# Loading and transposing the queries once, with the swapped half written by copies inside SBUF

## The chip, the cores and the metric

One core of one Trainium2 chip runs the whole program in a single launch. The metric is device time in microseconds (us) of that core. An engine is named as the profile does: PE is TensorE (PEld its weight loads), DVE is VectorE, ACT is ScalarE, POOL is GpSimd, SP is SyncE, which only issues DMAs here; SPq and ACTq are the queues of DMA issues of SP and ACT. HBM is the memory off the core, SBUF the memory on it, PSUM the memory that matmuls write to.

## The reference

Three layers in a row, all in float32, for 4 batches, 8 heads, 576 positions and a head width of 64 (model width 512):

```python
scores = scale * np.matmul(q, k.transpose(0, 1, 3, 2))
thresh = np.max(scores, axis=-1, keepdims=True) - tau
scores = np.where(scores >= thresh, scores, -1000000000.0)
...
attn = attn / (np.sum(attn, axis=-1, keepdims=True) + 1e-09)
return np.matmul(attn, v).astype(np.float32)
...
mixed = np.real(X).astype(np.float32)
u = x + mixed
...
ch = np.maximum(un @ w_ch1, 0.0) @ w_ch2
return (u + ch).astype(np.float32)
...
gate = 1.0 / (1.0 + np.exp(-gate_pre))
val = x @ w_val
return (gate * val @ w_out).astype(np.float32)
```

`X` is the Fourier transform of the attention's output over positions and model width, `un` is `u` normalised over the model width (512, with 2048 in the middle of the second layer), and `gate_pre` a causal convolution of 5 taps over positions.

The change touches only how the queries come to the first matmul.

## The kernel before, in words

**Stages.** The attention works on 16 pairs of heads (4 pairs to a batch). While it runs, TensorE's spare time is filled with other work of the attention and with the Fourier transform of the batches that are done, and the other engines convert the weights of the layer behind from 64-bit words to two float32r parts. When the attention's tiles end (about 380 us), the multilayer perceptron begins with its first block of columns, still mixed with the last batch's Fourier transform and the conversion of the rest of the weights; from about 505 us it and the gated output run matmul after matmul.

**Scores.** A pair has nine tiles of 128 query rows: four for each head and one that holds the last 64 rows of both. `emit_s` (L563) makes one tile's scores. The 576 keys of a head are held in two halves of 288: `kt[0:64, h]` holds keys 0 to 287 of head h (transposed, so that the 64 partitions are the head width), `kt[64:128, h]` keys 288 to 575. The matmul of a half contracts over the partitions that this half lies on, so the queries of the head must lie on partitions 0 to 63 and again on 64 to 127. Before the change both copies come from HBM: `qn` has an axis of 2 (`j`) that is loaded with the same rows twice, and a transpose of `[128 rows, 2 x 64]` gives both copies at once, in `qt[:, h]`.

**Loads.** `load_qk` (L179) issues nine DMAs per pair on SP, in this order: two for the keys (`kn`), one for the last 32 rows of each half of the keys (`tn`), two for the last 64 query rows (`tn` again, twice the same), four for the other 512 query rows (`qn`, two heads, each twice). For pair 0 the queries go through ACT's queue and are loaded once, and POOL copies them (L206). `nat_p` has one buffer, so the loads of a pair wait for the transposes of the pair before.

**Preparation.** `g_prep_qk` (L247) is a generator that makes a pair's `kt` and `qt`: four transposes of keys into one PSUM tile, copied out by DVE (L264); two transposes of 96 rows into a second, copied out by ACT (L271) and DVE (L272); then for each head four transposes of queries into a tile of its own, copied out by ACT with the scale (L279). At its `yield "sync"` it waits until its tiles are read, and issues the loads of the next pair.

**Order.** The attention is written step by step, two tiles a step, 72 steps and a few to drain. `ORDER` (L34) is the order of the pieces in a step: M0 and M1 are the row maxima (DVE, L585), E0 and E1 the exponentials (ACT, L592), K0 and K1 the masks (DVE, L602), S2 and S3 the scores of the next two tiles (PE, L573), N0 and N1 the division by the sum (POOL, L609), T0 and T1 the transposes of the probabilities (PE, L643), WD, WA, WP one operation of the weight conversion. F1 and F2 issue the ACT copies of the filler tiles that are ready, H1 to H3 the copies that follow on other engines. P1 and P2 call the filler (L678), which gives PE up to 1250 and 1350 ns of queued work, in this order of queues: `g_tail` (transposes of the probabilities' last columns, L623), the preparation of the next pair, the Fourier transform (L242), one mean, and the products with the values `g_pv` (L318). A filler tile needs room: its generator's `yield "room"` lets it go on only while at most one filler tile is open (`state["open"] <= 1`), so at most two tiles are started until copies have emptied them, however short they are. A pair's preparation is queued in the step in which the pair before begins, about four steps ahead of its first scores.

The lines that the prediction follows:

```python
def ready(g):
    ...
    if kind == "sync":
        return state["read"] >= put
    return state["open"] <= 1
...
queues = [(q_prep, q_tail, q_mean, q_pv, q_fft)[i] for i in QORD]
```

Where the whole `while` loop at L669 runs the preparation of pair 0, nothing else is on the engines.

Of the kernel before, what the change touches and what calls it, by code (L numbers as in the profile page):

```python
# [11 lines left out]
F32 = mybir.dt.float32  # L12
# [3 lines left out]
AF = mybir.ActivationFunctionType  # L16
# [5 lines left out]
B, H, S, D = 4, 8, 576, 64  # L22
# [4 lines left out]
MAIN, TAIL = 512, 64  # L27
HALF = S // 2
# [106 lines left out]
def attention_fft(tc, right, ps_f, a, u_d, dram, conv_w, hooks):  # L135
    nc = tc.nc
    PE, DVE, ACT, POOL, SP = nc.tensor, nc.vector, nc.scalar, nc.gpsimd, nc.sync
    left, right1 = ExitStack(), ExitStack()
    with ExitStack() as right2, ExitStack() as right2b, ExitStack() as right3, ExitStack() as right4, ExitStack() as scores, ExitStack() as turned:
        def pool(stack, name, bufs, side="right", **kw):  # L140
            return stack.enter_context(tc.tile_pool(name=name, bufs=bufs, side=side, **kw))
# [13 lines left out]
        nat_p = pool(left, "nat", 1, side="left")  # L155
# [3 lines left out]
        ident = id_p.tile([128, 128], F32, name="ident")  # L159
        tau = const.tile([128, 1], F32, name="tau_sb")  # L160
        atau = const.tile([128, 1], F32, name="atau")
        alpha = const.tile([128, 1], F32, name="alpha")
# [16 lines left out]
        def load_qk(p, second=SP):  # L179
            b, hs = p // NP, slice(2 * (p % NP), 2 * (p % NP) + 2)  # L180
            kn = nat_p.tile([128, 2, 2, 2, D], F32, tag="kn", name="kn")
            qn = nat_p.tile([128, 2, 4, 2, D], F32, tag="qn", name="qn")
            tn = nat_p.tile([96, 2, 2, D], F32, tag="tn", name="tn")
            k, q = a["k"][b, hs].rearrange("h (g p) d -> p h g d", g=2), a["q"][b, hs]
            for j in range(2):
                SP.dma_start(out=kn[:, j], in_=k[j * 128:j * 128 + 128])
            SP.dma_start(out=tn[0:32], in_=k[256:HALF])

            def queries(h, j):
                second.dma_start(out=qn[:, h, :, j], in_=q[h, 0:MAIN].rearrange("(t p) d -> p t d", p=128))  # L190

            def last_queries():
                for j in range(2):
                    second.dma_start(out=tn[32:96, :, j], in_=q[:, MAIN:S].rearrange("h p d -> p h d"))

            if second is SP:
                last_queries()
                for h in range(2):
                    for j in range(2):
                        queries(h, j)  # L200
            else:
                for h in range(2):
                    queries(h, 0)
                    if h == 0:
                        last_queries()
                    POOL.tensor_copy(qn[:, h, :, 1], qn[:, h, :, 0])  # L206
            nat[p] = tn, kn, qn

        def load_v(p):
# [22 lines left out]
        def fill_tile():  # L232
            state["open"] += 1
            return ps_f.tile([128, 512], F32, tag="f", name="f")

        def done(first, *then):

            evacs.append((first, then))
            state["put"] += 1
# [7 lines left out]
        def g_prep_qk(p):  # L247

            tn, kn, qn = nat.pop(p)
            kt = qk_p.tile([128, 2, HALF], F32, tag="kt", name="kt")  # L250
            qt = qk_p.tile([128, 2, S], F32, tag="qt", name="qt")

            yield "room"
            f = fill_tile()
            for h in range(2):
                for j in range(2):
                    o = (2 * h + j) * 128
                    PE.transpose(f[:, o:o + 128], kn[:, j, h].rearrange("p g d -> p (g d)"), ident)
                    yield 121.0
            fk = f.rearrange("p (h k) -> p h k", h=2)  # L260
            if KEYS_ACT:
                done(lambda: ACT.activation(kt[:, :, 0:256], fk, AF.Copy))
            else:
                done(lambda: None, lambda: DVE.tensor_copy(kt[:, :, 0:256], fk))  # L264
            yield "room"
            f = fill_tile()
            for h in range(2):
                PE.transpose(f[:, h * 96:h * 96 + 96], tn[:, h].rearrange("p g d -> p (g d)"), ident[0:96, 0:96])
                yield 121.0
            fv = f[:, 0:192].rearrange("p (h k) -> p h k", h=2)  # L270
            done(lambda fv=fv: ACT.activation(qt[:, :, MAIN:S], fv[:, :, 32:96], AF.Identity, scale=alpha[:, 0:1]),  # L271
                 lambda fv=fv: DVE.tensor_copy(kt[:, :, 256:HALF], fv[:, :, 0:32]))  # L272
            for h in range(2):
                yield "room"
                f = fill_tile()
                for t in range(4):
                    PE.transpose(f[:, t * 128:(t + 1) * 128], qn[:, h, t].rearrange("p g d -> p (g d)"), ident)
                    yield 121.0
                done(lambda f=f, h=h: ACT.activation(qt[:, h, 0:MAIN], f, AF.Identity, scale=alpha[:, 0:1]))  # L279
            yield "sync"  # L280
            if 0 < p < NPAIR - 1:
                load_qk(p + 1)
            kq[p] = (qt, kt)
# [273 lines left out]
        def force(ready):  # L557
            while not ready():
                flush()
                advance_side()  # L560
                fill(1.0)

        def emit_s(g):  # L563
            p, h, i = tiles[g]
            force(lambda: p in kq)
            qt, kt = kq[p]
            s = ps_s.tile([128, 2, 512], F32, tag="s", name="s")
            for hh in ((h,) if h < 2 else (0, 1)):
                q = slice(i * 128, i * 128 + 128) if h < 2 else slice(MAIN, S)
                o = slice(0, 128) if h < 2 else slice(hh * 64, hh * 64 + 64)  # L570
                for c in range(2):
                    w = slice(c * 64, c * 64 + 64)
                    PE.matmul(out=s[o, c, 0:HALF], lhsT=qt[w, hh, q], rhs=kt[w, hh, :], start=True, stop=True)  # L573
            sc[g] = s

        def p_view(g):
# [81 lines left out]
        LAG = 4  # L658
        SP.dma_start(out=ident, in_=a["ident"])
        load_qk(0, ACT)  # L660
        DVE.tensor_scalar(out=atau, in0=tau, scalar1=-1.0, scalar2=None, op0=ALU.mult)
        DVE.tensor_tensor(out=atau, in0=atau, in1=tau, op=ALU.max)
        for t in negs:
            for j in range(2):
                DVE.tensor_copy(t[:, j, 1:2], atau)
        DVE.tensor_scalar(out=alpha, in0=tau, scalar1=0.0, scalar2=float(D) ** -0.5,
                          op0=ALU.is_ge, op1=ALU.mult)
        q_prep.append(g_prep_qk(0))
        while q_prep:  # L669
            fill(1e9)  # L670
            flush()
        load_qk(1)
        emit_s(0)
        emit_s(1)

        spare = 0.0
# [6 lines left out]
        for u in range(NT // 2 + 3):  # L683
            t = 2 * u
            on = [x for x in (t, t + 1) if x < NT]
            state["tile"] = t
            for x in on:
                p, h, i = tiles[x]
                if h == 0 and i == 0 and p + 1 < NPAIR:
                    q_prep.append(g_prep_qk(p + 1))  # L690
                if h == 0 and i == 2:
                    if p == 0:
                        side.append(g_prep_v(0))
                    if p + 1 < NPAIR:
                        side.append(g_prep_v(p + 1))
# [30 lines left out]
            def S2():  # L726
                if t + 2 < NT: emit_s(t + 2)
# [816 lines left out]
```

## Time and profile before

| | us |
|---|---|
| median of 3 runs | 938.17 |
| lowest, highest | 937.34, 938.41 |
| span of the profiled execution, first to last instruction | 936.0 |

No time of its own is given for the profiled execution beyond its span, so durations are summed against 936.0, and the median is 938.17 - 936.0 = 2.2 us above it (other executions, timed around the whole launch).

| engine | busy us of 936.0 |
|---|---|
| PE | 884.3 (94%) |
| PEld | 708.0 (76%) |
| DVE | 553.5 (59%) |
| ACT | 451.2 (48%) |
| POOL | 368.0 (39%) |

How to read it: a matmul's duration in the profile is its latency, and matmuls overlap, so the cost of one in a row is the row's length divided by their count. A line of the timeline merges neighbouring instructions of one kind: start, length, engine, line of the kernel, operation, what it writes and reads, count, and in brackets the idle time of the engine before it and what ended it.

### The profile page before, as it was taken

What the parts mean: (1) busy time and instruction counts of PE and PEld (TensorE: products, weight loads), DVE (VectorE), ACT (ScalarE), POOL (GpSimd) and SP (SyncE); (2) the same over time, 40 slices, a digit from 0 to 9 for tenths busy, and PEclk for the clock granted to TensorE, in tenths of its full rate; (3) what the DMA queues carried; (4) which work ended last, traced back from release to release, by engine and by line L of the source; (5) the groups of instructions that cost most, each with busy time, mean ns of one, the idle gap of its engine ahead of it and who ended that gap; (6) DMA issues with size and microseconds to landing.
All of it is one profiled execution on the core that took longest, in us unless ns stands there. A gap on an engine that the chain in (4) does not pass through costs nothing. (4 is left out here: it accounts for less than half of the span.)

```text
span 936.0 us, 14888 instructions
## 1 busy us (share of the span) xinstructions
PE 884.3 (94%) x5232; PEld 708.0 (76%) x5232; DVE 553.5 (59%) x1240; ACT 451.2 (48%) x915; POOL 368.0 (39%) x451
## 2 busy tenths in 40 slices
PE   6988899999999999799988999999999999999998
PEld 4555576657665765488866999999999989998897
DVE  5888888888887767316577243442412275735750
ACT  3778777777777766526355123213211313224432
POOL 2465645584467545612553321312111011037421
PEclk9999999999999999999999999999999999999999
DMA  6775545556555732587259524212110050233111
GB/s 151 190 193 129 165 119 167 154 163 173 164 142 172 193 92 72 178 314 234 89 204 351 204 91 130 79 46 85 52 66 1 1 178 3 91 130 122 70 46 68
DMA packets 135283, 123.34 MB, mean 132 GB/s; under 512 B 85686, under 2 KB 99238, under 8 KB 135208
## 3 DMA queue, kind: packets, MB, share of 16 engines
q1 hardware_dynamic: 126760, 97.57, 33.7%
q0 software_dynamic: 6960, 24.49, 8.5%
q8 instruction: 42, 0.69, 0.3%
q10 hardware_dynamic: 1488, 0.33, 0.2%
q14 instruction: 33, 0.27, 0.1%
HBM read 89.85 MB, written 37.22 MB: 136 GB/s over the span
## 5 line engine op out<-in xcount | busy, mean ns | idle before, releaser
L1072 DVE SCALAR_TENSOR_TENSOR hl<-h,hh 128x448 fp32r<-128x448 f32 (+1 forms) x80 | 51.0, 637 | 209.6 <-ACT hh L1071 209.6
L1071 ACT ACTIVATE hh<-h 128x448 fp32r<-128x448 f32 (+1 forms) x80 | 44.4, 555 | 262.9 <-PE h L1068 262.9
L609 POOL TENSOR_SCALAR p<-p,su 128x576 f32<-128x576 f32 x144 | 109.9, 769 | 91.1 <-DVE su L699 71.5
L602 DVE SCALAR_TENSOR_TENSOR p<-s,thr,e 128x576 f32<-128x576 f32 x144 | 112.6, 815 | 39.8 <-ACT e L592 21.9
L573 PE MATMUL s<-kt,qt 64*128 64x288 f32 (+1 forms) x640 | 101.3, 448 | 24.8 <-DVE p L602 24.8
L1084 PE MATMUL c<-hl,w1h 128*128 128x448 f32 (+1 forms) x320 | 118.9, 371 | 0.5 <-DVE hl L1072 0.5
L1084 PE MATMUL c<-hh,w1h 128*128 128x448 f32 (+1 forms) x320 | 118.8, 371 | 0.0
L1084 PE MATMUL c<-hh,w1l 128*128 128x448 f32 (+1 forms) x320 | 118.7, 371 | 0.0
L592 ACT ACTIVATE e<-s,neg 128x576 f32<-128x576 f32 x144 | 99.4, 737 | 28.5 <-DVE neg L585 27.9
L585 DVE TENSOR_REDUCE neg<-s 128x1 f32<-128x576 f32 x144 | 101.6, 745 | 14.5 <-PE s L573 14.5
L573 PEld LDWEIGHTS s<-kt,qt 64*128 64x128 f32 (+1 forms) x640 | 46.2, 178 | 66.3 <-issue 24.3
L652 ACT ACTIVATE m<-t 128x512 f32<-128x512 f32 x144 | 84.6, 588 | 6.5 <-PE t L643 6.4
L1068 PE MATMUL h<-unh,w0l 128*128 128x448 f32 (+1 forms) x320 | 81.9, 378 | 5.9 <-POOL w0l L106 5.9
L1068 PE MATMUL h<-unh,w0h 128*128 128x448 f32 (+1 forms) x320 | 80.5, 373 | 3.6 <-DMA w0h<-e_h 3.2
L318 PE MATMUL f<-m,v 128*64 128x320 f32 (+1 forms) x512 | 80.4, 415 | 1.5 <-ACT m L652 1.2
L1068 PE MATMUL h<-unl,w0h 128*128 128x448 f32 (+1 forms) x320 | 81.2, 376 | 0.0
L643 PE MATMUL t<-ident,p 128*128 128x128 f32 x576 | 77.9, 278 | 2.9 <-POOL xf L348 1.9
L643 PEld LDWEIGHTS t<-ident,p 128*128 128x128 f32 x576 | 64.3, 142 | 18.4 <-issue 10.3
L1068 PEld LDWEIGHTS h<-unh,w0l 128*128 128x128 f32 x320 | 60.8, 191 | 14.0 <-POOL w0l L106 7.2
L1068 PEld LDWEIGHTS h<-unh,w0h 128*128 128x128 f32 x320 | 59.9, 188 | 11.8 <-DMA w0h<-e_h 3.7
L1068 PEld LDWEIGHTS h<-unl,w0h 128*128 128x128 f32 x320 | 61.2, 191 | 7.2
L1084 PEld LDWEIGHTS c<-hl,w1h 128*128 128x128 f32 x320 | 60.1, 188 | 7.7 <-DVE hl L1072 0.9
(219 smaller groups left out, 1538.7 us busy)
## 6 DMA issues: line engine op xcount, KB each, us to landing
raw<-in_moe_w_ch POOLq DMA_DIRECT2D x32, 512.0 KB, 4.9
qn<-in_q SPq DMA_DIRECT2D x60, 128.0 KB, 2.9
xs<-xt SPq DMA_DIRECT2D x16, 288.0 KB, 4.1
e_h<-cx SPq DMA_DIRECT2D x18, 256.0 KB, 4.1
e_l<-ct SPq DMA_DIRECT2D x18, 256.0 KB, 5.3
w0h<-e_h SPq DMA_DIRECT2D x18, 256.0 KB, 6.7
w0l<-e_l SPq DMA_DIRECT2D x18, 256.0 KB
w1h<-e_h SPq DMA_DIRECT2D x18, 256.0 KB, 5.3
```

The costliest lines, as they stand in the source:

```text
L318: PE.matmul(out=f[h * 64:h * 64 + 64, 0:n], lhsT=w, rhs=r, start=(t == 0), stop=(t == 4))
L573: PE.matmul(out=s[o, c, 0:HALF], lhsT=qt[w, hh, q], rhs=kt[w, hh, :], start=True, stop=True)
L585: DVE.tensor_reduce(out=neg[i][:, j, 0:1], in_=sc[g][:, :, 0:HALF], axis=AX.XY, op=ALU.max, negate=True)
L592: ACT.activation(e, sc[g][:, :, 0:HALF], AF.Exp, bias=neg[g // 2][:, g % 2, 0:1], scale=1.0)
L602: DVE.scalar_tensor_tensor(out=p_view(g).rearrange("p (a b) -> p a b", a=2), in0=sc.pop(g)[:, :, 0:HALF], scalar=thr[g // 2][:, j], in1=ex ...
L609: POOL.tensor_scalar(out=v, in0=v, scalar1=su, scalar2=1.0, op0=ALU.mult, op1=ALU.mult)
L643: PE.matmul(out=f[:, t, :], lhsT=pv[:, t * 128:(t + 1) * 128], rhs=ident, is_transpose=True, start=(t == 0), stop=(t == 3))
L652: tq.append(lambda: ACT.activation(o, fv, AF.Copy))
L1068: PE.matmul(out=f[:, 0:n], lhsT=ww[:, k * 128:(k + 1) * 128], rhs=x[:, k, 0:n], start=(i == 0), stop=(i == 3 * KB - 1))
L1071: ACT.activation(hh, f[:, 0:n], AF.Relu)
L1072: DVE.scalar_tensor_tensor(out=hl, in0=f[:, 0:n], scalar=0.0, in1=f32(hh), op0=ALU.max, op1=ALU.subtract)
L1084: PE.matmul(out=ch[c][o][:, 0:n], lhsT=ww[:, o * 128:(o + 1) * 128], rhs=x, start=(at_ == 0 and i == 0), stop=(at_ == FB - 1 and i == 2))
```

## The change

Each query row is loaded once. The two heads of a pair lie side by side in `qn[:, t]` (`[128, 2 x 64]`), so one transpose puts head 0 on partitions 0 to 63 and head 1 on partitions 64 to 127 of `qt[:, 0]`. The last rows of both heads and both key halves' ends go through one transpose of `[128, 128]` (`rest`) instead of two of 96 rows. Queries and `rest` are transposed before the keys instead of behind them. Then, at "sync", two DMAs on SP write `qt[:, 1]`, which is `qt[:, 0]` with its two halves of the partitions exchanged, and `emit_s` reads `qt[w, hh ^ c]`. A pair's nine loads become seven, and the two copies come ahead of the next pair's loads in SP's queue. For pair 0 all of this happens before the first scores; POOL's two copies there are gone, and the ends of the keys take two DMAs on SP instead of one.

```diff
--- before.py
+++ after.py
             kn = nat_p.tile([128, 2, 2, 2, D], F32, tag="kn", name="kn")
-            qn = nat_p.tile([128, 2, 4, 2, D], F32, tag="qn", name="qn")
-            tn = nat_p.tile([96, 2, 2, D], F32, tag="tn", name="tn")
+            qn = nat_p.tile([128, 4, 2, D], F32, tag="qn", name="qn")
+            tn = nat_p.tile([128, 2, D], F32, tag="tn", name="tn")
             k, q = a["k"][b, hs].rearrange("h (g p) d -> p h g d", g=2), a["q"][b, hs]
             for j in range(2):
                 SP.dma_start(out=kn[:, j], in_=k[j * 128:j * 128 + 128])
-            SP.dma_start(out=tn[0:32], in_=k[256:HALF])
-
-            def queries(h, j):
-                second.dma_start(out=qn[:, h, :, j], in_=q[h, 0:MAIN].rearrange("(t p) d -> p t d", p=128))
...
+            for h in range(2):
+                second.dma_start(out=qn[:, :, h], in_=q[h, 0:MAIN].rearrange("(t p) d -> p t d", p=128))
+            for h in range(2):
+                SP.dma_start(out=tn[h * 32:h * 32 + 32], in_=k[256:HALF, h])
+            second.dma_start(out=tn[64:128], in_=q[:, MAIN:S].rearrange("h p d -> p h d"))
             nat[p] = tn, kn, qn
...
+            def queries(o, order):
+                f = fill_tile()
+                for t in range(4):
+                    PE.transpose(f[:, t * 128:(t + 1) * 128], order(qn[:, t]), ident)
+                    yield 121.0
+                done(lambda f=f: ACT.activation(qt[:, o, 0:MAIN], f, AF.Identity, scale=alpha[:, 0:1]))
+
+            def rest():
+                f = fill_tile()
+                PE.transpose(f[:, 0:128], tn.rearrange("p h d -> p (h d)"), ident)
+                yield 121.0
+                done(lambda f=f: ACT.activation(qt[:, 0, MAIN:S], f[:, 64:128], AF.Identity, scale=alpha[:, 0:1]),
+                     lambda f=f: DVE.tensor_copy(kt[:, :, 256:HALF], f[:, 0:64].rearrange("p (h k) -> p h k", h=2)))
+
+            yield "room"
+            yield from queries(0, lambda t: t.rearrange("p h d -> p (h d)"))
+            yield "room"
+            yield from rest()
             yield "room"
             f = fill_tile()
             for h in range(2):
...
-            yield "room"
-            f = fill_tile()
-            for h in range(2):
-                PE.transpose(f[:, h * 96:h * 96 + 96], tn[:, h].rearrange("p g d -> p (g d)"), ident[0:96, 0:96])
-                yield 121.0
...
-            for h in range(2):
-                yield "room"
-                f = fill_tile()
-                for t in range(4):
-                    PE.transpose(f[:, t * 128:(t + 1) * 128], qn[:, h, t].rearrange("p g d -> p (g d)"), ident)
-                    yield 121.0
-                done(lambda f=f, h=h: ACT.activation(qt[:, h, 0:MAIN], f, AF.Identity, scale=alpha[:, 0:1]))
             yield "sync"
+            for c in range(2):
+                SP.dma_start(out=qt[64 - c * 64:128 - c * 64, 1], in_=qt[c * 64:c * 64 + 64, 0])
             if 0 < p < NPAIR - 1:
                 load_qk(p + 1)
...
-                    PE.matmul(out=s[o, c, 0:HALF], lhsT=qt[w, hh, q], rhs=kt[w, hh, :], start=True, stop=True)
+                    PE.matmul(out=s[o, c, 0:HALF], lhsT=qt[w, hh ^ c, q], rhs=kt[w, hh, :], start=True, stop=True)
```

## Rows read from the trace of the kernel before

**Rows 1.** The page's first part: span, and busy time of TensorE.
```profile
span 936.0 us, 14888 instructions
PE 884.3 (94%) x5232; PEld 708.0 (76%) x5232; DVE 553.5 (59%) x1240; ACT 451.2 (48%) x915; POOL 368.0 (39%) x451
```
**Rows 2.** Busy time in stretches: one batch of 18 steps; the perceptron's first block.
```profile
core 0: us, PE busy (x) PEld busy (x) DVE busy (x) ACT busy (x) POOL busy (x), PEclk, DMA share, GB/s
222.83:319.02 96.19, 91.28 (x673) 61.63 (x671) 78.97 (x191) 70.99 (x154) 56.76 (x76) 1.00 0.56 162
...
395.00:505.50 110.50, 101.16 (x477) 82.92 (x475) 61.51 (x103) 51.45 (x95) 43.36 (x48) 0.97 0.67 229
```
**Rows 3.** The same view of single steps of that batch, with a preparation.
```profile
239.56:243.96 4.40, 3.77 (x30) 2.82 (x29) 4.17 (x13) 3.89 (x9) 2.65 (x4) 1.00 0.93 264
243.96:248.57 4.61, 3.56 (x26) 2.08 (x25) 3.72 (x9) 3.87 (x9) 1.46 (x3) 1.00 0.73 156
...
259.85:265.23 5.38, 4.58 (x36) 3.34 (x34) 4.45 (x12) 5.05 (x13) 2.69 (x5) 1.00 0.57 170
...
293.88:298.55 4.67, 3.79 (x28) 2.71 (x29) 4.05 (x10) 4.35 (x11) 4.61 (x8) 1.00 0.42 161
```
**Rows 4.** The timeline through the first two of these steps.
```profile
239.81 0.25 PEld L268 LDWEIGHTS f<-ident,tn 96*128 96x128 f32 x2
...
240.87 1.50 PE L573 MATMUL s<-kt,qt 64*128 64x288 f32 x8 [0.63 <-DVE p L602]
...
242.29 0.86 PEld L277 LDWEIGHTS f<-ident,qn 128*128 128x128 f32 x8 [0.39 <-DVE kt L272]
...
242.52 1.40 DVE L585 TENSOR_REDUCE neg<-s 128x1 f32<-128x576 f32 x2
...
242.99 1.26 ACT L279 ACTIVATE qt<-f,alpha 128x512 f32<-128x512 f32 x2 [0.18 <-PE f L277]
...
244.15 1.37 ACT L592 ACTIVATE e<-s,neg 128x576 f32<-128x576 f32 x2
...
245.86 1.49 PE L573 MATMUL s<-kt,qt 64*128 64x288 f32 x8 [1.05 <-DVE p L602]
```
**Rows 5.** Instructions that write the tile qt: count, duration min/median/max in ns.
```profile
L279 ACT ACTIVATE qt<-f,alpha x32: 658/682/691, 8.6 to 340.1; 128x512 f32<-128x512 f32 x32
L271 ACT ACTIVATE qt<-f,alpha x16: 349/367/370, 7.1 to 337.3; 128x128 f32<-128x128 f32 x16
```
**Rows 6.** The timeline of the first 10 us.
```profile
1.19 0.96 SPq L186 DMA_DIRECT2D kn<-in_k  x2
...
4.61 0.45 PE L258 MATMUL f<-ident,kn 128*128 128x128 f32 x1 [4.61 <-DMA kn<-in_k]
...
5.69 0.90 PE L258 MATMUL f<-ident,kn 128*128 128x128 f32 x3 [0.64 <-DMA kn<-in_k]
...
6.58 0.40 POOL L206 COPY qn<-qn 128x256 f32<-128x256 f32 x1 [1.06 <-DMA qn<-in_q]
...
7.42 1.94 PE L277 MATMUL f<-ident,qn 128*128 128x128 f32 x8 [0.39 <-POOL qn L206]
...
8.55 0.69 ACT L279 ACTIVATE qt<-f,alpha 128x512 f32<-128x512 f32 x1 [1.11 <-PE f L277]
9.29 0.51 PEld L573 LDWEIGHTS s<-kt,qt 64*128 64x128 f32 x4 [0.33 <-ACT qt L279]
```
**Rows 7.** DMAs: issues, size and median us to landing; landing of the tile tn.
```profile
qn<-in_q SPq DMA_DIRECT2D x60, 128.0 KB, 2.9
...
xd<-xs SPq DMA_DIRECT2D x7, 288.0 KB, 9.0
...
DMA to landing us min/median/max: 2.2/3.0/5.5
```
**Rows 8.** The timeline where pair 9 is prepared and first used.
```profile
201.11 1.26 ACT L279 ACTIVATE qt<-f,alpha 128x512 f32<-128x512 f32 x2
...
202.09 3.65 SPq L186 DMA_DIRECT2D kn<-in_k  x2
...
210.95 0.30 PEld L573 LDWEIGHTS s<-kt,qt 64*128 64x128 f32 x4 [0.44 <-issue]
```

More of the change, by code (lines that the diff above doesn't have):

```diff
@@ L186, in load_qk @@
                 SP.dma_start(out=kn[:, j], in_=k[j * 128:j * 128 + 128])
-            SP.dma_start(out=tn[0:32], in_=k[256:HALF])
-            def queries(h, j):
-                second.dma_start(out=qn[:, h, :, j], in_=q[h, 0:MAIN].rearrange("(t p) d -> p t d", p=128))
[L192 to L197, printed above, removed]
-                for h in range(2):
-                    for j in range(2):
-                        queries(h, j)
-            else:
-                for h in range(2):
[L203 to L206, printed above, removed]
+            for h in range(2):
[3 more added lines that the diff above has]
+            second.dma_start(out=tn[64:128], in_=q[:, MAIN:S].rearrange("h p d -> p h d"))
             nat[p] = tn, kn, qn
@@ L264, in g_prep_qk @@
                 done(lambda: None, lambda: DVE.tensor_copy(kt[:, :, 0:256], fk))
-            yield "room"
-            f = fill_tile()
-            for h in range(2):
-                PE.transpose(f[:, h * 96:h * 96 + 96], tn[:, h].rearrange("p g d -> p (g d)"), ident[0:96, 0:96])
-                yield 121.0
[L270 to L273, printed above, removed]
-                yield "room"
-                f = fill_tile()
-                for t in range(4):
-                    PE.transpose(f[:, t * 128:(t + 1) * 128], qn[:, h, t].rearrange("p g d -> p (g d)"), ident)
-                    yield 121.0
-                done(lambda f=f, h=h: ACT.activation(qt[:, h, 0:MAIN], f, AF.Identity, scale=alpha[:, 0:1]))
             yield "sync"
+            for c in range(2):
+                SP.dma_start(out=qt[64 - c * 64:128 - c * 64, 1], in_=qt[c * 64:c * 64 + 64, 0])
             if 0 < p < NPAIR - 1:
```

## The prediction

> **What bounds the kernel now.** I read the page's first part, then the busy time by stretches, then single steps, then the timeline inside a step. TensorE is busy 884.3 of 936.0 us [rows 1], but that share mixes stages. The change acts in the attention, and a batch there takes 96.19 us for 18 steps, in which TensorE is busy 91.28 us: 4.91 us idle [rows 2]. So most steps are held by TensorE, whose scores and transposes leave room for filler work, and a few are not. The reader should look at the steps in which a pair is prepared or has just been prepared. The four of that batch shown are idle for 0.63, 1.05, 0.80 and 0.88 us [rows 3], 3.36 us in all, or two thirds of the batch's idle time. The timeline says why: the scores wait for DVE's mask, 0.63 us in the first step and 1.05 us in the second [rows 4]. In these steps the filler had nothing to give, since a preparation opens two PSUM tiles at a time, two of them short, and no third may be opened. There the chain maxima, exponentials, masks, scores is the bound.
>
> In the second of them this chain contains a piece of the change. The first maximum (the first of two in a line of 1.40 us, so 0.70 us) ends at 242.52 + 0.70 = 243.22, but the exponentials start at 244.15, because ACT first empties two tiles of queries, 242.99 to 244.25 [rows 4]. That is 0.9 us in the chain.
>
> **What is removed on TensorE.** Eight transposes of queries take 0.86 us in a row, 0.107 each; two of 96 rows take 0.25, 0.125 each [rows 4]. A pair goes from 14 transposes to 9: 4 x 0.107 + 0.125 = 0.55 us less. For the 14 pairs prepared among other steps (2 to 15) that is 7.7 us if TensorE is the bound wherever the filler work lands. In the steps held by the chain it is not, but there ACT's part counts: one copy of 682 ns less [rows 5], and since the queries are now transposed first, their copy is issued in the same step, behind its exponentials, so up to 0.9 us leaves the chain of the following step. I price a pair at 0.55 us on average, by TensorE or by the chain: **7.7 us**. Its bounds are 0 (the freed time is filled or waits elsewhere) and 0.55 plus half of a preparing step's mean idle time, 3.36 / 4 / 2 = 0.42, if the room that two tiles fewer leave lets a block of the Fourier transform start earlier: 0.97 x 14 = 13.6 us. I stay at 0.55, since every batch waits for its last pair before its transform can start, and an earlier start is not seen in any row.
>
> **What moves to other engines.** DVE copies the same keys as before, now a step later; between the maxima and the masks it waits for exponentials anyway, so I cost this at nothing. If that cover went, it would be one key copy in the chain. The copy of the last queries has half its columns and costs less than the 367 ns it took [rows 5]. Matmuls that read `hh ^ c` have the same shapes.
>
> **The DMAs.** Each pair issues nine as before: seven loads and two copies. SP holds the copies until ACT has written `qt`, and behind them wait the next pair's loads, then whatever the transform and the weight conversion store. The loads have the rest of the pair to land. The scores wait for the copies. No row shows a copy inside SBUF. The nearest are the query loads of 128 KB, median 2.9 us to landing; the fastest small one took 2.2, and the slowest kind a median of 9.0 for 288 KB [rows 7]. A copy has 64 x 576 x 4 bytes = 144 KB, nearest to the query load, so I take 2.9. Cover: a preparation comes about two to three steps ahead. The tightest pairs are 9 and 13, behind the store of a batch's transform. For pair 9 ACT's copies end at 201.11 + 1.26 = 202.37 and the first scores load weights at 210.95, 8.6 us later [rows 8]; pair 13 repeats it a batch later, the other pairs have 14 us. So I cost the copies at nothing inside the attention.
>
> At the start there is no cover. Two loads issued together (0.96 us) fed TensorE at 4.61 and 5.69: the second landed 1.08 us behind the first [rows 6]. The first scores began at 9.29, when ACT's first copy was done; transposes had begun at 7.42, behind POOL's copy of a load that landed at 6.58, and the way from there to 9.29 took 1.9 us [rows 6]. Without POOL's copy and with the second head's load issued earlier, transposes begin between 5.7 and 6.6, so ACT ends between 7.6 and 8.5, with the copy of the last rows (under 0.37) at up to 8.9. A copy adds 2.2 to 2.9, and the second half of the scores starts at 9.8 to 11.8. That is 0.5 to 2.5 us later than 9.29; I take **+1.3 us**, and for the second copy up to 1.08 more as an upper end. Pair 1's loads are also held back by the copies, which may cost the first step about as much again, but its queries no longer delay the second step's exponentials; I set these two against each other.
>
> The Trainium skill, SBUF — State Buffer, section "Can I just issue two DMAs to hit both halves?", answers no: transfers to the two halves of the partitions serialize. By that the second copy would land a whole copy after the first, not 1.08 us, so the start would cost 1.8 us more and the sum would give 933.6; no run here shows such a copy.
>
> **What follows behind the attention.** In the perceptron's first block, 395.0 to 505.5, TensorE is idle 110.50 - 101.16 = 9.3 us [rows 2]. Its weights are being converted there, in turns that the program deals out step by step, so an earlier attention moves them along; I cost this at nothing. If the gain lies in filler work instead of in shorter steps, TensorE merely arrives earlier at weights that aren't ready, and the stall eats it. That is the second rival.
>
> **Sum.** -7.7 + 1.3 = -6.4 us: the span goes from 936.0 to 929.6. The median lies 2.2 us above the profiled span, so 938.17 - 6.4 = **931.8 us**.
>
> **Rivals.** *The idle time is used too.* The preparation now has three filler tiles, not four, and two of them fill their tile, so that a block of the transform fits into the same step. For it: 3.36 us of idle time a batch sit just there. Against it: some of these waits are the chain's own length. Price: 14 x 0.42 = 5.9 us more, **925.9 us**.
>
> *The gain is taken back behind.* The steps keep their length, as each still gives out its 2600 ns of filler while there is any, and the time saved comes out as filler work that is done earlier, ahead of the 9.3 us of stalls. For it: the steps held by TensorE are filled to their budget. Against it: a batch shows 4.91 us idle, so the filler does run out. Only the start's 1.3 us and about as much gain would be left: **938.2 us**.
>
> *The copies come late.* At pairs 9 and 13 SP's queue is slow: two loads took 3.65 us to issue [rows 8], so transfers ahead are clogging it. If the copies are slowed as much and land like the slowest kind, the second one arrives at 202.37 + 3.65 + 1.08 + 9.0 = 216.1, 5.1 us after 210.95. Twice that, 10.3, against the 6.4 gained gives **942.1 us**. It decides from a landing of more than 8.6 us after ACT's copy on; the other pairs need 14. Against it: 9.0 is for twice the bytes, between two places in HBM and SBUF at the busiest time.
>
> **How the numbers follow.** A measurement of this kernel tells a change from none at about 0.2%, 1.9 us. Chances: the forecast, 0.45; idle time used as well, 0.23; taken back, 0.17; copies late, 0.15. The first two are faster, 0.68; the third is the same, 0.17; the last is slower, 0.15. The range goes from 938.17 - 13.6 - 1.0 = 923.5 (the upper bound of the gain, with the start at no loss and a little more from the chain) to 940.5: it holds the first three cases, the start at its upper end among them, and leaves out most of the late copies. The forecast's own range is 928 to 936.
>
> **What would show it.** Right: 80 transposes and 16 query copies fewer on PE and ACT; the exponentials of the step behind a preparation starting right after the first maximum; the idle times of those steps at 1.05 us smaller; the attention's last step some 6 us earlier; no score waiting for a DMA after the first tile; the first scores' second half at 10 to 11.8. Wrong: scores that wait for the copies in pairs 9 and 13; steps of the same length, with the stalls before 505 longer; query transposes, now the first of a preparation, that wait for their load.

## The result, and the profile after

The kernel got slower, not faster: its median went from 938.06 us to 945.55, a ratio of 1.0073 with a 95% interval of [1.0057, 1.0089]; 931.8 us had been forecast, in a range up to 940.5. The median of 945.55 counts a fourth execution of 4419.32 us, which the ratio leaves out; without it the median is 945.01 us. The profiled execution has a span of 941.7 us, 5.7 above that of before [rows 1].

The page's first lines of the kernel after:

```profile
span 941.7 us, 14728 instructions
...
PE 881.7 (94%) x5152; PEld 697.7 (74%) x5152; DVE 548.8 (58%) x1240; ACT 444.2 (47%) x899; POOL 366.2 (39%) x449
```

The 80 transposes are gone, TensorE is busy 2.6 us less than in [rows 1], and ACT has 16 instructions fewer than the 915 of before. So the work did shrink, and the time grew.

Where it grew is read from three stretches: the 71 steps of the attention (from the first row threshold to the last), what follows up to 430.5 us ahead of the end, and those 430.5 us. First the kernel before, then after; columns as in [rows 2]: length, then busy time of PE, PEld, DVE, ACT and POOL with their instructions, clock, DMA share, GB/s.

```profile
12.43:381.66 369.23, 341.46 (x2479) 226.60 (x2478) 298.42 (x732) 267.92 (x572) 210.87 (x284) 1.00 0.55 154
381.66:505.50 123.84, 110.74 (x548) 88.85 (x548) 65.83 (x112) 59.89 (x114) 53.37 (x61) 0.97 0.65 222
505.50:936.00 430.50, 425.35 (x2180) 387.98 (x2180) 183.04 (x370) 119.45 (x225) 102.74 (x102) 1.00 0.26 88
```

```profile
14.16:388.93 374.77, 338.48 (x2408) 217.22 (x2408) 294.34 (x732) 261.86 (x557) 209.95 (x284) 0.99 0.53 152
388.93:511.20 122.27, 112.62 (x550) 89.14 (x548) 66.04 (x112) 59.54 (x113) 53.12 (x61) 0.96 0.65 221
511.20:941.70 430.50, 425.28 (x2180) 387.92 (x2180) 182.20 (x370) 119.72 (x226) 102.94 (x102) 1.00 0.26 89
...
229.79:329.05 99.26, 90.73 (x655) 59.08 (x654) 76.45 (x193) 69.68 (x150) 56.76 (x77) 1.00 0.54 160
```

In the last stretch PE's busy time is the same to 0.1 us. The start costs 14.16 - 12.43 = 1.73 us, the steps 374.77 - 369.23 = 5.54, and the stretch behind gives 1.57 back: 5.7 in all. In the steps TensorE is busy 2.98 us less and idle 36.29 instead of 27.77, so 8.5 us of new idle time outweigh the work that went. The batch of [rows 2] has its counterpart in the last row: 99.26 us for 18 steps instead of 96.19, idle 8.53 instead of 4.91. In the steps the granted clock is not the reason: it is 1.00 and 0.99, and the one stretch at the lower level that only the kernel after has there lies in a step as long as before (from 85.51 us, at a mean clock of 0.70: 5.66 us in both kernels).

What ends that idle time is in the page's costliest groups, before and then after:

```profile
L602 DVE SCALAR_TENSOR_TENSOR p<-s,thr,e 128x576 f32<-128x576 f32 x144 | 112.6, 815 | 39.8 <-ACT e L592 21.9
L573 PE MATMUL s<-kt,qt 64*128 64x288 f32 (+1 forms) x640 | 101.3, 448 | 24.8 <-DVE p L602 24.8
```

```profile
L592 DVE SCALAR_TENSOR_TENSOR p<-s,thr,e 128x576 f32<-128x576 f32 x144 | 112.9, 815 | 48.9 <-PE f L613 26.0
L563 PE MATMUL s<-kt,qt 64*128 64x288 f32 (+1 forms) x640 | 105.8, 454 | 34.2 <-DVE p L592 29.2
```

The scores wait for the masks, as before and 4.4 us longer (29.2 instead of 24.8), but the masks now wait above all for `f` of L613, which are the tail transposes: the transposes of a row's last columns of probabilities, work that the filler deals out. A mask writes a row of probabilities into one of four buffers (`PBUFS = 4`), and the buffer is free only when the tail transpose has read the row that is in it. The waits of DVE's mask for it (us in all, number, longest), in the whole of the kernel before and then of the kernel after, there with two other waits of DVE:

```profile
DVE p L602 <- PE f L623: 9.0, 5, 2.7
```

```profile
DVE p L592 <- PE f L613: 26.0, 16, 2.6
DVE kt L250 <- ACT qt L249: 10.6, 11, 3.3
DVE cx L96 <- DMA e_h<-cx: 4.0, 2, 3.1
```

Five waits of 9.0 us became sixteen of 26.0; twelve stand in steps that had none before. The second row is new with the change: DVE's copy of the last keys (L250) waits for ACT's copy of the last queries (L249), and the maxima of the next tile stand behind it. One of the sixteen, in the timeline of the kernel after:

```profile
290.48 2.10 PE L308 MATMUL f<-m,v 128*64 128x320 f32 x13
290.50 0.82 DVE L592 SCALAR_TENSOR_TENSOR p<-s,thr,e 128x576 f32<-128x576 f32 x1 [1.51 <-ACT e L582]
...
293.31 0.63 PE L613 MATMUL f<-ident,p 128*64 128x128 f32 x4
...
293.97 0.82 DVE L592 SCALAR_TENSOR_TENSOR p<-s,thr,e 128x576 f32<-128x576 f32 x1 [2.64 <-PE f L613]
...
294.85 0.76 PE L563 MATMUL s<-kt,qt 64*128 64x288 f32 x4 [0.22 <-DVE p L592]
```

The filler gave TensorE a long run of products with the values, and the tail transposes came behind them; the second mask waited 2.64 us, the scores of the next tile behind it. That step takes 8.67 us. It took 7.66 before, where it had a wait of 2.53 us of the same kind, one of the five.

The copies themselves are seldom waited for. The whole attention has two such waits, both at the start, here in the timeline from the query transposes on:

```profile
6.63 1.08 PE L241 MATMUL f<-ident,qn 128*128 128x128 f32 x4 [6.63 <-DMA qn<-in_q]
...
7.75 0.69 ACT L243 ACTIVATE qt<-f,alpha 128x512 f32<-128x512 f32 x1 [4.89 <-PE f L241]
...
8.50 1.11 PE L261 MATMUL f<-ident,kn 128*128 128x128 f32 x4 [0.56 <-ACT qt L243]
8.67 1.19 SPq L270 DMA_DIRECT2D qt<-qt  x2
...
9.65 0.69 DVE L267 COPY kt<-f 128x512 f32<-128x512 f32 x1 [0.74 <-PE f L261]
...
10.39 0.50 PEld L563 LDWEIGHTS s<-kt,qt 64*128 64x128 f32 x2 [1.18 <-DVE kt L267]
...
11.05 0.50 PEld L563 LDWEIGHTS s<-kt,qt 64*128 64x128 f32 x2 [0.16 <-DMA qt<-qt]
...
11.76 0.74 PEld L563 LDWEIGHTS s<-kt,qt 64*128 64x128 f32 x4 [0.21 <-DMA qt<-qt]
```

The first scores wait for DVE's copy of the keys, which are now the last to be transposed; the exchanged halves cost 0.16 and 0.21 us more.

### The profile page after: what moved, and what is told of

The parts are those of the page before. It is cut to its first block, busy times and chain, and to the rows that moved or that the text cites. A ratio compares the mean times of both kernels' runs of the same rounds, so it can differ in the third digit from the quotient of the medians.

```text
span 941.7 us, 14728 instructions
## 1 busy us (share of the span) xinstructions
PE 881.7 (94%) x5152; PEld 697.7 (74%) x5152; DVE 548.8 (58%) x1240; ACT 444.2 (47%) x899; POOL 366.2 (39%) x449
## 5 line engine op out<-in xcount | busy, mean ns | idle before, releaser
L563 PE MATMUL s<-kt,qt 64*128 64x288 f32 (+1 forms) x640 | 105.8, 454 | 34.2 <-DVE p L592 29.2
L106 POOL TENSOR_TENSOR ct<-raw 128x512 fp32r<-128x512 f32 x26 | 28.7, 1110 | 101.9 <-DVE raw L102 51.5
```

The lines of the kernel that those rows point to most:

```text
L563: PE.matmul(out=s[o, c, 0:HALF], lhsT=qt[w, hh ^ c, q], rhs=kt[w, hh, :], start=True, stop=True)
```

## The experiments

Two theories stood against each other. A: fewer transposes in another order give the filler another deal (a portion is the TensorE time that the filler gives out in one go; a preparation leaves 5 x 121 = 605 ns of it to other work, and holds three tiles, not four), and masks then wait for row buffers. B: the copies, or what stands behind them on SP's queue, cost the time. A third candidate was the order of the preparation. All were timed beside the kernel before, whose median then was 936.9 to 938.2 us; a ratio is against those executions, with a 95% interval in brackets, and is not exactly the quotient of the two medians. Steps are counted from 1, each from one row threshold to the next.

**Without the copies** (`e1_no_copies`); the scores then read the uncopied half for both heads, which mixes the heads:

```diff
-            for c in range(2):
-                SP.dma_start(out=qt[64 - c * 64:128 - c * 64, 1], in_=qt[c * 64:c * 64 + 64, 0])
...
-                    PE.matmul(out=s[o, c, 0:HALF], lhsT=qt[w, hh ^ c, q], rhs=kt[w, hh, :], start=True, stop=True)
+                    PE.matmul(out=s[o, c, 0:HALF], lhsT=qt[w, 0, q], rhs=kt[w, hh, :], start=True, stop=True)
```

> The changed kernel without its two copies inside SBUF; the scores read the uncopied half of qt for both heads, so head and queries are mixed and the output is not the reference's. Every other instruction and the filler's deal stay as in the changed kernel (945.6 us). If the deal is the cause (theory A: the filler hands out TensorE's work in other portions, and the masks wait for transposes of the probabilities' last columns that are dealt later), the time stays at 943 to 946, less the copies' 1.2 us at the start, so 942 to 946. If the copies are (theory B: SP's queue and the DMA engines), it falls to 931 to 937. If the order is (theory C: queries ahead of keys), it stays too.

Measured: 942.58 us, ratio 1.0055 [1.0037, 1.0073]. Between this and the kernel after lie 0.18%, some 1.7 us, and the intervals overlap. The masks' wait for the tail transposes is the same to the tenth (26.0 us, 16 times). This is in A's range (942 to 946), far from B's (931 to 937). The copies are the smaller part of the loss at most.

**Keys first again** (`e2_keys_first`): keys, last rows, queries, the rest of the change as it is.

```diff
-            yield from queries(0, lambda t: t.rearrange("p h d -> p (h d)"))
-            yield "room"
-            yield from rest()
-            yield "room"
             f = fill_tile()
...
+            yield "room"
+            yield from rest()
+            yield "room"
+            yield from queries(0, lambda t: t.rearrange("p h d -> p (h d)"))
```

> The changed kernel with the keys' transposes first again, then the last rows, then the queries; copies as in the change. A: the deal is still made of three short segments, so the steps are again uneven: 939 to 947. B: 943 to 947, as the copies are the same. C: 935 to 939, back at the kernel before or a little under.

Measured: 953.92 us, 1.0192 [1.0166, 1.0218], slower still and above the range of every theory, with 27.6 us of masks waiting for tail transposes. Going back to the old order doesn't give the loss back. It moves it: eight steps, in which DVE's copy of the last keys waits for ACT in the kernel after, are 0.55 to 1.21 us shorter, and the steps right behind them 0.45 to 2.85 us longer.

**The old portions** (`e3_same_deal`): keys first, and the filler is told what the four portions cost before, the last of them empty, so that every other piece of filler work falls where it fell before.

```diff
+            yield "room"
+            yield from rest()
+            yield "room"
+            yield from queries(0, lambda t: t.rearrange("p h d -> p (h d)"))
+            yield "room"
+            state["open"] += 1
+            for _ in range(4):
+                yield 121.0
+            done(lambda: None)
```

> The changed kernel with keys first, and the filler told that the preparation costs what it cost before: the transpose of the last rows is charged twice, and an empty fourth portion (four charges of 121 ns, one place of the two open tiles, no instruction) stands where the second head's queries stood. So every step gets the same portions in the same places as in the kernel before, with 5 transposes and one ACT copy fewer a pair, and with the copies. A: faster than the kernel before by part of the 6.4 us that the prediction summed, 930 to 936. B: slower than before by what the copies cost, 940 to 946. C: 935 to 939.

Measured: 945.2 us, 1.0097 [1.0071, 1.0123]. This is B's number (940 to 946); A had asked for 930 to 936. Step by step the trace shows both what the change saves and what the copies cost. Nine of the steps behind a preparation are 0.29 to 0.58 us shorter than before, near the 0.55 of the prediction. But its first threshold is 2.5 us later than before, step 27 takes 9.27 us instead of 6.21, and SP's queue now stands behind ACT's query copies. The waits of SP's queue in this kernel, and the timeline at that step:

```profile
SPq L276 <- ACT qt L243: 70.7, 13, 18.2
```

```profile
123.58 1.14 SPq L276 DMA_DIRECT2D qt<-qt  x2
...
130.88 8.59 SPq L929 DMA_DIRECT2D e_h<-cx  x1
...
140.04 0.41 SPq L929 DMA_DIRECT2D e_h<-cx  x1
...
146.44 0.43 DVE L96 TENSOR_SCALAR cx<-raw 128x512 int32<-128x512 int32 x1 [3.15 <-DMA e_h<-cx]
```

With the queries last in the preparation, the copies wait for ACT on SP's queue (5.8 us here, 18.2 at the longest); the next pair's loads and the transform's transfers queue behind them, and then the weight conversion's stores of `e_h`. DVE, which must overwrite the stored tile, stands for 3.15 us in the middle of the attention.

**A fifth row buffer** in the kernel after (`p5_after`) and, as the control, in the kernel before (`p5_before`):

```diff
-PBUFS = 4
+PBUFS = 5
```

> The changed kernel with five buffers for the rows of probabilities instead of four, so that a mask needs the transposes of the last columns of five row tiles back, not four. A: most of the masks' wait (26 us of DVE's idle time, put down to those transposes) goes, and the time falls to 933 to 941. B and C: 943 to 946, since copies and order are untouched.

> The kernel before with a fifth buffer for the probabilities' rows, the control of the run of the kernel after with five. If the masks' wait for the tail transposes is what the change brought (26.0 us in 16 waits after, 9.0 us in 5 before), the fifth buffer has little to give here: 935.5 to 938, and the kernel after with five buffers (939.4) stays behind it. If the fifth buffer is worth as much to any deal of the filler, it takes the 6 us that it took from the kernel after: about 931.5.

Measured: after 939.41 us, 1.0023 [1.0010, 1.0037]; before 940.33 us, 1.0036 [1.0018, 1.0054]. With four buffers the change costs 0.73%; with five, the times with and without it can't be told apart. The first lies in A's range, the second in neither. The stretches of the kernel after with five buffers, then of the kernel before with five:

```profile
14.20:382.84 368.64, 339.20 (x2413) 220.91 (x2415) 295.37 (x731) 260.36 (x557) 209.78 (x285) 0.99 0.55 155
382.84:507.10 124.26, 113.39 (x551) 90.20 (x552) 67.65 (x114) 61.64 (x115) 52.93 (x61) 0.96 0.64 222
```

```profile
12.43:378.28 365.85, 340.34 (x2477) 226.27 (x2476) 296.67 (x732) 267.52 (x572) 207.22 (x282) 0.99 0.55 155
378.28:508.00 129.72, 114.71 (x562) 91.52 (x561) 67.95 (x113) 61.55 (x116) 54.88 (x63) 0.96 0.64 221
```

In the kernel after the fifth buffer takes 6.1 us out of the steps, and the masks' waits for tail transposes fall from 26.0 us to 3.3; this is theory A's mechanism taken away. What is left is TensorE's idle time of 368.64 - 339.20 = 29.44 us, where the control has 365.85 - 340.34 = 25.51: of the 8.5 us of new idle time about half goes with the row buffers, and 3.9 stay. DVE's waits of the last keys' copy for ACT stay too (11.7 us in 11); whether they are the other half is not shown. The control brought a surprise: its steps are shorter too, by 3.4 us, but the stretch behind grows by 5.9, so that it ends later than the kernel before. So it is the stretch behind that makes the two times equal, not the steps: those of the kernel after are 2.8 us longer. In that stretch the perceptron's first block waits 4.4 us for `w0h`, weights that aren't converted yet, instead of 3.2, and TensorE is busy 4 us longer, at a granted clock of 0.96 instead of 0.97; by these rows the clock is worth 0.04 x 129.72 - 0.03 x 123.84 = 1.5 us of it, an estimate. Why more than the gain comes back was not tried.

**The copies on ACT's queue**, in the kernel after (`e4_act_queue`) and with the old portions (`e5_same_deal_act`):

```diff
-                SP.dma_start(out=qt[64 - c * 64:128 - c * 64, 1], in_=qt[c * 64:c * 64 + 64, 0])
+                ACT.dma_start(out=qt[64 - c * 64:128 - c * 64, 1], in_=qt[c * 64:c * 64 + 64, 0])
```

> The kernel after, with the two copies of a pair issued by ACT instead of SP: SP's queue no longer stands behind ACT's query copies (16.7 + 11.6 us of waiting after). Theory A (the deal of the filler, masks wait for row buffers): nothing changes in the attention's steps, 943.5 to 946, masks waiting for tails still near 26 us. Theory B (the copies hold up the loads and stores behind them on SP's queue): the long steps of 8.7 to 9.0 us shorten by 1 to 1.5 us each, 941 to 942.5, like the run without copies (942.6). If issuing costs ACT its own time inside the chain (two issues took SP 1.19 us at the start), up to 16 x 1.2 = 19 us more: up to 963.

> The run with the filler's old portions (keys, rest, queries, an empty fourth portion; 945.2), with the copies issued by ACT. There SP's queue stood 64.5 us behind ACT's query copies, 18.2 at the longest, and the loads and the conversion's stores stood behind that. Theory B (that standing queue cost what the shorter preparations gained): DVE's wait of 3.15 us for a store and the scores' waits for keys go, 0.5 us stay saved at each of 14 pairs, with a start that is 3.5 us later: 934 to 939. Theory A alone (the deal, which is the old one here): no change by the queue, 944 to 947. Issuing on ACT inside the chain: up to 19 us more.

Measured: 945.95 us, 1.0102 [1.0079, 1.0125], and 943.37 us, 1.0065 [1.0044, 1.0087]. The first is A's number: nothing is gained, and the masks still wait 25 us for tail transposes. One step, the 45th, does get 2.1 us shorter (6.87 instead of 8.96), since DVE waits 0.87 us there for a store of `e_h` and not 3.13; TensorE had other work during that wait (busy 8.66 of the 8.96 us), and later steps lose as much. The second lies in neither range. With the old portions the second store of `e_h` comes 1.9 us earlier and DVE no longer waits for it in step 27 (timeline):

```profile
138.12 0.32 SPq L929 DMA_DIRECT2D e_h<-cx  x1
144.47 0.43 DVE L96 TENSOR_SCALAR cx<-raw 128x512 int32<-128x512 int32 x1
```

The steps are 373.30 - 370.47 = 2.8 us shorter than in `e3_same_deal`, but the intervals of the two ratios overlap, and steps 41 and 59 are 1.9 and 1.0 us longer than before: there TensorE waits 1.5 and 1.3 us for the load of `tn`, whose query rows are now loaded last. The granted clock is 0.72 in step 41 and 0.80 in the next, which is 1.9 us longer too, so that the load's part can't be told from the clock's. So a standing queue cost what step 27 shows; that it cost `e3_same_deal` all of its gain is not shown.

**Old portions, ACT's queue and five buffers** (`e7_deal_act_p5`, the last diff with `PBUFS = 5`):

> The run before it in this call with a fifth row buffer as well. Theory A: the old portions leave few waits for row buffers (12.0 us in 9 with the copies on SP), so the fifth buffer gives 1 to 3 us: 932 to 938. If the fifth buffer takes 5 to 6 us from any kernel: 928 to 934, faster than the kernel before.

Measured: 938.14 us, 1.0012 [1.0000, 1.0024], at the edge of A's range and above the 928 to 934 that a fifth buffer worth 5 to 6 us would have given. The steps take 361.63 us, 7.6 less than before and 4.2 less than the control with five buffers; the start is 3.46 us later (first threshold at 15.89), and the stretch behind takes 128.88 us, 5.0 more.

**The deal alone** (`d1_before_portions`, `d2_before_portions`, `d1_after_portions`): the work is untouched, the two portions of a step's filler are shifted by 100 ns.

```diff
-FILLS = (1250, 1350, 600, 1050)
+FILLS = (1350, 1250, 600, 1050)
```

(`d2_before_portions` has 1150 and 1450.)

> The kernel before with the two portions of a step's filler at 1350 and 1250 ns instead of 1250 and 1350: the same work, the same sum, only dealt otherwise. Theory A (the deal alone is worth several us, since it decides which tail transposes free a row buffer in time): the time moves by 3 us or more, to 941 to 948 if this kernel's portions had been fitted to its work, and the masks' wait for the tail transposes moves with it. If the deal is worth little, so that the loss lies in what the change itself does: 936.5 to 939.

> The kernel before with portions of 1150 and 1450 ns, a shift of 100 the other way. Theory A: 940 to 948, as for the shift the first way. Little worth in the deal: 936.5 to 939.

> The kernel after with portions of 1350 and 1250 ns. Theory A (its loss of 7 us is a matter of the deal, not of the copies): the time moves by 3 us or more either way, 938 to 950. If the copies or the work behind them are the loss: 943.5 to 946.5.

Measured: 949.33 us, 1.0115 [1.0098, 1.0132]; 936.14 us, 0.9977 [0.9965, 0.9989]; and for the kernel after 960.69 us, 1.0242 [1.0222, 1.0261], against its 1.0073. The first and the third lie above the ranges of both theories, the second below. That the deal alone is worth more than the whole change is shown. But the shift the other way made the same kernel 0.23% faster, so a loss doesn't follow from any other deal; and the deal works through more than one wait: in `d1_before_portions` the masks wait less for tail transposes than before, 6.6 us, and the loss sits in two steps of 11.66 and 13.07 us. In the first of them, timeline:

```profile
182.70 0.79 POOL L453 TENSOR_TENSOR xd<-xd,dd 128x289 f32<-128x289 f32 x1 [8.93 <-DMA xd<-xs]
183.47 0.75 POOL L609 TENSOR_SCALAR p<-p,su 128x576 f32<-128x576 f32 x1
...
184.28 0.66 PE L643 MATMUL t<-ident,p 128*128 128x128 f32 x4 [4.67 <-POOL p L609]
```

A piece of the Fourier transform that waits 8.93 us for its transfer was dealt onto POOL's queue ahead of a division by the sums, and TensorE's transposes of that row waited 4.67 us for it. The 960.69 us come in the same way. The longest step of `d1_after_portions`, by stretches and by timeline:

```profile
195.63:208.40 12.77, 8.04 (x41) 5.45 (x41) 4.19 (x11) 5.12 (x12) 10.90 (x15) 0.60 0.34 114
```

```profile
197.12 0.80 POOL L443 TENSOR_TENSOR xd<-xd,dd 128x289 f32<-128x289 f32 x1 [11.93 <-DMA xd<-xs]
...
198.69 1.12 PE L633 MATMUL t<-ident,p 128*128 128x128 f32 x4 [4.95 <-POOL p L599]
```

In the kernel after this step, the 37th, takes 5.44 us. Here POOL waits 11.93 us for the transfer and TensorE 4.95 us for POOL, and TensorE's granted clock is 0.60 in the mean, so most of the step ran at the lower of its two levels (1.2 and 2.4 GHz). Over all steps the clock is 0.97, against 0.99 in the kernel after, so a part of this loss can be the lower clock behind such a stop, and not the wait alone; how much is not shown.

**The start repaired** (`e8_start`): `e7_deal_act_p5`, with pair 0's exchanged queries made as before, by POOL's copies into a tile `qs` and four more transposes; for this pair only the last 64 query rows (columns 512 to 575 of `qt`) are copied by DMA.

```diff
+                if p == 0:
+                    POOL.tensor_copy(qs[:, :, 1 - h], qn[:, :, h])
...
+            if p == 0:
+                yield from queries(0, lambda t: t.rearrange("p h d -> p (h d)"))
+                yield "room"
+                yield from queries(1, lambda t: t.rearrange("p h d -> p (h d)"), qs)
+                yield "room"
+                yield from rest()
+            else:
...
+            n0 = MAIN if p == 0 else 0
```

> The fastest variant of the change so far (the old portions, copies issued by ACT, five row buffers; 938.1 with a first threshold 3.46 us later than before and steps 7.6 us shorter), with the first pair's exchanged queries made as before, by POOL's copies and four more transposes. If the start was the rest of the loss: the first threshold at 12.4 to 13.0 instead of 15.9, so 934.6 to 935.5, faster than before. If an attention that ends earlier is given back behind, as in the kernel before with five buffers (steps 3.4 us shorter, the stretch behind 5.9 longer): the perceptron's first block waits that much longer for its weights and the time stays at 937 to 939.

Measured: 933.16 us, 0.9953 [0.9932, 0.9975], faster than the kernel before and than the kernel after, and below both ranges. Its stretches:

```profile
13.10:373.02 359.92, 334.60 (x2402) 220.21 (x2403) 300.40 (x732) 260.08 (x557) 208.47 (x283) 0.99 0.56 158
373.02:500.00 126.98, 112.99 (x553) 89.69 (x552) 66.61 (x112) 59.79 (x114) 53.44 (x63) 0.96 0.61 212
```

The steps take 359.92 us, 9.3 less than before. Against the control with the same five buffers (365.85) they are 5.9 us shorter. 1.7 of these are one step, 6.78 us in the control at a granted clock of 0.90, that is as long in the kernel before as here (5.09 and 5.08 us, clock 1.00), so they are not the change's. The other 4.2 us, 0.30 for each of 14 pairs, lie mostly in steps behind a preparation; `e7_deal_act_p5` has the same 4.2. One of them, the 47th, in the control and then in this kernel, by stretches and by timeline:

```profile
242.93:247.54 4.61, 3.56 (x26) 2.08 (x25) 3.72 (x9) 3.87 (x9) 1.46 (x3) 1.00 0.81 189
```

```profile
242.55 0.68 ACT L279 ACTIVATE qt<-f,alpha 128x512 f32<-128x512 f32 x1
...
243.12 1.37 ACT L592 ACTIVATE e<-s,neg 128x576 f32<-128x576 f32 x2
243.95 0.82 DVE L602 SCALAR_TENSOR_TENSOR p<-s,thr,e 128x576 f32<-128x576 f32 x1 [0.86 <-ACT e L592]
```

```profile
240.05:244.09 4.04, 3.13 (x22) 1.66 (x21) 3.72 (x10) 3.30 (x8) 1.47 (x3) 1.00 0.57 142
```

```profile
239.67 0.73 ACT L599 ACTIVATE e<-s,neg 128x576 f32<-128x576 f32 x1
...
240.22 0.47 ACTq L287 DMA_DIRECT2D qt<-qt  x1
240.29 0.74 ACT L599 ACTIVATE e<-s,neg 128x576 f32<-128x576 f32 x1
240.49 0.82 DVE L609 SCALAR_TENSOR_TENSOR p<-s,thr,e 128x576 f32<-128x576 f32 x1 [0.28 <-ACT e L599]
```

ACT no longer copies a second tile of queries ahead of the exponentials, the mask waits 0.28 us for them instead of 0.86, and the step is 0.57 us shorter.

## Why the prediction was wrong

**The gain of a pair** had the right kind, about half the size, and an assumption that failed. "I price a pair at 0.55 us on average, by TensorE or by the chain" took every step's other filler work to stay where it was. Where that holds (the old portions), single steps behind a preparation are 0.3 to 0.58 us shorter, by the chain as forecast, but over 14 pairs it is 4.2 us against the control with the same five buffers: 0.30 a pair, not 0.55. With the start repaired the kernel stands at 0.9953 against 1.0036 for that control, 0.0083 x 938 = 7.8 us (their intervals, [0.9932, 0.9975] and [1.0018, 1.0054], lie apart). That this is near the 7.7 of the forecast is luck: by the two traces 1.7 us are the control's step at the lower clock and 129.72 - 126.98 = 2.7 the stretch behind the attention, and the start takes 0.7. In the kernel after the assumption does not hold. Of the 7.7 us TensorE's busy time in the steps shows 2.98, and 8.5 us of new idle time were added by a different deal: the steps grew by 5.54 us instead of shrinking by 7.7.

**The failing step** is thus the pair's price of 0.55 us with its lower bound of 0: a new deal was thought of only as a gain ("the idle time is used too") or as nothing. The trace of before held the row that spoke against it, five masks that waited 9.0 us for tail transposes, and I did not read it. These transposes are filler work that frees a buffer on the critical path, so work freed elsewhere in the filler changes when they run. The fifth buffer shows that about half of the new idle time hangs on them.

**The key copies** were a second cost put at nothing: "between the maxima and the masks it waits for exponentials anyway, so I cost this at nothing" looked at DVE's copy of the keys, and not at what that copy waits for. In the kernel after DVE stands 10.6 us in 11 such waits for ACT's copy of the last queries, and nine steps that hold one are 0.12 to 1.28 us longer than before. What they cost by themselves is not shown, as in the run with the keys first those waits went and the steps behind grew.

**The DMAs.** "I cost the copies at nothing inside the attention" was right of the waits: no score waited for a copy after the first tile, and pairs 9 and 13 did not either. The tile `qt` of the kernel after:

```profile
DMA to landing us min/median/max: 2.3/2.4/8.6
```

The median is 2.4 us where I took 2.9. The copies, and what I costed at nothing behind them on SP's queue, are worth the 1.7 us by which the kernel without copies is better, with intervals that overlap. At the start the scores that wait for the second copy begin 11.76 - 11.05 = 0.71 us behind those that wait for the first. The Trainium skill (SBUF — State Buffer, "Can I just issue two DMAs to hit both halves?") says that two such transfers serialize. The prediction made a whole landing of that, 2.9 us, and the trace doesn't agree with this reading; the rule itself it leaves open, since the two issues, 1.19 us for both, already stand about 0.6 us apart.

**The start** was forecast at +1.3 us (0.5 to 2.5) and is +1.73 at the first threshold, +0.8 two steps later (23.65 against 22.83). The size is right, the reason only in part: the exchanged halves wait 0.4 us in all, and the rest is the wait for the key copy, "now a step later", which at the start has no cover.

**Behind the attention** I costed the stall at nothing. For this change the stretch even gave 1.57 us back, but two kernels whose attention ends earlier, at 377.52 and 378.28 us, lose 5.0 and 5.9 us there, and of the 9.3 us by which the steps of `e8_start` are shorter (it ends earliest, at 373.02) 3.1 are taken back. So the rival "the gain is taken back behind" has something to it where the steps do get shorter, but how much is taken back does not follow from how early the attention ends.

**The rival that ended slower** had the right sign by another mechanism: the copies were to come late for pairs 9 and 13, and there the scores waited for no DMA.

**Open**: why the stretch behind grows by more than the steps gained with five buffers in the kernel before, what makes the other half of the new idle time, and how much of `e3_same_deal`'s loss is SP's queue.

## What to carry to other kernels

In a kernel whose idle time is filled by a dealer of work, less work is not less time: first find what the filler's pieces release (buffers that a mask or a score waits for), and read how often that wait already occurs before the change. To judge the saving itself, run it with the old deal, with the released portion left empty, and measure what a shift of the deal alone is worth; here 100 ns moved the kernel before by -0.23% one way and by +1.15% the other, and the second is more than the change's +0.73%. A DMA that waits for a compute engine should not stand ahead of loads and stores that others need on the same queue.

## What the runs showed of the hardware

Copies of 144 KB inside SBUF landed in a median of 2.4 us in the kernel after, but of 4.1 us both in `e4_act_queue` (same deal, ACT's queue) and in `e3_same_deal` (another deal, SP's queue). So neither the size nor the queue alone sets it; it was not expected that the same copy takes 1.7 times as long by when and from where it is issued. Issuing them on ACT's queue took 0.47 us for the first in the timeline of `e8_start`, with an exponential of 0.74 us running beside it, and the up to 19 us that had been feared did not appear: the kernel after is at 1.0102 [1.0079, 1.0125] with ACT's queue and at 1.0073 [1.0057, 1.0089] with SP's.
